# Turning the data on TensorE instead of in the transfers, in a one-core S5 and H3 kernel

## The chip, the core and the metric

The kernel runs on one core of a Trainium2 chip. A core has five engines that each work through their own instructions in order: TensorE (PE, matrix products, with its weight loads listed apart as PEld), VectorE (DVE), ScalarE (ACT), GpSimd (POOL) and SyncE (SP), which here only issues transfers. Sixteen DMA engines carry the transfers. An engine waits for another only where a semaphore says so. Data lie in SBUF (128 partitions) or in PSUM, where TensorE puts its results. The metric is the device time of one execution in microseconds (us); lower is better. The kernel before took 339.0 us, the median of three runs (338.59 to 339.09).

## What is computed

Two kinds of layer alternate on a tensor `x` of 2048 tokens by 640 channels. `_layernorm` has no weights.

```python
def _A_ref(x, Lambda_re, Lambda_im, B_re, B_im, C_re, C_im, log_dt, Dskip):
    ...
    Lam_bar = jnp.exp(dt * Lam)
    Bu = jnp.einsum("bld,pd->blp", x + 0j, B_bar)
    for t in range(L):
        h = Lam_bar[None, :] * h + Bu[:, t, :]
        hs.append(h)
    y = 2.0 * jnp.einsum("blp,dp->bld", hseq, Cmat).real + x * Dskip[None, None, :]

def _B_ref(q, k, v, shift_k, ssm_k, ssm_D):
    for t in range(ks):
        k_shift = k_shift + k_pad[:, t:t + S, :] * shift_k[:, ks - 1 - t][None, None, :]
    kv = k_shift * v
    ...
    y_f = kv_f * kf_f[None, :, :, :]
    y = irfft2(y_f)[:, 0, :S, :] + kv * ssm_D[None, None, :]
    return q * y

x = A_x
x = x + _A_ref(_layernorm(x), ...)
x = x + _B_ref(_layernorm(x), B_k, B_v, B_shift_k, B_ssm_k, B_ssm_D)
x = x + _A_ref(_layernorm(x), ...)
x = x + _B_ref(_layernorm(x), B_k, B_v, B_shift_k, B_ssm_k, B_ssm_D)
```

The long convolution `y` of a B layer depends on k, v and the two filters alone, not on `x`. So the kernel computes it once, keeps it in DRAM (`ysd`), and both B layers multiply by it.

## The kernel before

**Order.** Nothing is scheduled while the kernel is being built. Each piece of work is a named task of the class `Sched` (`add`), and the string `ORDER` (lines 59 to 141) lists all 896 tasks in one order. `run` emits them so, and each engine gets its own tasks in that order. A suffix gives the engine where a task has a choice: `/a` ACT, `/d` DVE, `/p` POOL. `PLACE` (from line 143) fixes the address of each buffer in one large SBUF area, `arena`, and the PSUM banks. The times that tasks carry (`c_mm`, `c_act`, `c_tt`) are not used when the kernel is built.

**Set-up.** `y_table_tasks` (line 998) makes the sine and cosine tables `Cf`, `Sf`, `NSf` for the forward spectrum, and `Ci`, `Si` as their turned copies by two DMA transposes (line 1047). Two negated copies, `NSi` and `NCi` (lines 1051 and 1053), follow on DVE. `a_setup_tasks` makes the weights of the A layers. A warm-up of 18 matmuls (line 1468) comes first on TensorE.

**The convolution.** The 640 channels go in five blocks of 128 (`kb`, `qd`). `kv_tasks` (line 1142) loads a block of k with a DMA transpose (line 1209) and a block of v plainly (line 1198), forms the short shift filter on TensorE (line 1227) and multiplies by v on DVE (line 1243). `y_pass` (line 1249) then takes kv, turned by another DMA transpose (line 1329), and the filter `ssm_k` (line 1311), through stage A (line 1272) and stage B (lines 1294 to 1296), whose results are copied out of PSUM by `evac` (line 290 on ACT, line 292 on DVE). The spectra are multiplied on DVE (lines 1350 to 1354). For block 0, which `PW_PE` names, the last two of these four operations are left out, and TensorE does them by a doubled number of products. The inverse stage (line 1376) uses `Ci`, `Si`, `NSi` as stationary operands and the spectrum as moving ones; its result `T` is turned by a DMA transpose (line 1389) into `TT`, TensorE applies `HA` (line 1404), and the block goes to `ysd` (line 1414).

**The A layers.** `ALayer.chunk` works on 512 tokens, four chunks per layer. After the layer norm, four `id` tasks (lines 696 and 698) write the normalised tokens in bf16, and one DMA transpose, task `tu` (line 726), turns them all. Tasks `bq` and `bp` (lines 750 and 765) multiply by B, `eq` and `ev` copy out of PSUM, `ri`, `sc` and `ro` (lines 803, 804, 820) run the recurrence on DVE, `hx` (line 875) takes a difference, `cp` (line 901) multiplies by C, and `xe` (line 909 on ACT, line 911 on DVE) adds up and gives the new `x`. Where `xe` is on ACT, TensorE adds the residual as well.

**The B layers.** `b_chunk` (line 917) normalises (`u`), multiplies by `ysd` (`mm`, line 959) and adds (`m`, lines 948, 980, 982). The last chunk of the last layer goes in four groups of one quarter; the output is stored after each second quarter (line 930).

Of the kernel before, what the change touches and what calls it, by code (L numbers as in the profile page):

```python
# [17 lines left out]
P = 128  # L18
L = 2048
# [18 lines left out]
PW_PE = (0,)  # L38
PW_PARTS = 1
VN = 1  # L40
KVS = ()
# [18 lines left out]
a_ldB1 a_ldB0 yt_io8 yt_ph8 kv_dsl kv_kd yq0_kl a_pl a_ti yt_h0 yt_io0 kv_pd2/p yt_f0 kv_lk0 kv_k0 yt_ph0 yt_f2 kv_d0  # L60
kv_lv0 warm kv_k1 a_b01:2 yt_sin8 xl0 yq1_kl kv_lk1 a_p0 kv_lv1 yt_sin0 yt_f3 a_b0e1:2/a a_p1 a_b00:4 a_b00:2 yt_neg8
kv_pd4/d kv_k2 yt_f4 kv_pd0/p a_p2 yq0_ka a_b0e0:4/a a_b01:3 yq0_KA:m0 a_b0e0:2/a a_p3 a_b00:3 a_b0e1:3/d yq0_KA:e0/d
kv_pd3/d kv_d1 kv_d2 a_p4a a_p4 kv_ds0 kv_ds1 a_dd yt_h1 kv_ds4 kv_ds3 kv_ds2 a_b00:1 a_b0e0:3/a a_b0e0:1/a a_b01:0
yt_neg0 a_b0e1:0/a a_b00:0 a_b0e0:0/a yq0_KA:m3 yq0_KA:e3/a yq0_KA:m2 kv_mm0:1 yq0_KA:e2/d kv_pd1/d a_ta yq0_KA:m1
a_b01:4 yq0_KA:e1/a kv_mm0:0 a_b0e1:4/a kv_ev0:1 a_t0 kv_ev0:0 yq0_vl a_ldC0 xl2 a_ldC1 a_p5a a_p5b yq0_KB:m0
yq0_KB:e0/a yq0_KB:m2 yq2_kl yt_Ci kv_lk2 yq0_KB:e2/a yt_Si a_p6 kv_lv2 yq1_ka a_f A1c0_ln_bn:1/d a_lamd/d yq1_KA:m1
yq1_KA:e1/a xl1 yq1_KA:m2 yq0_KB:m3 yq1_KA:m3 kv_mm1:0 yq1_KA:e3/a a_b01:1 yq1_KA:e2/a yq0_KB:e3/a kv_ev1:0 yt_h2
a_b0e1:1/a yt_h3/p a_t1 kv_mm1:1 kv_ev1:1 a_b11:3 yq0_VA:m2 a_b1e1:3/d yq0_VA:e2/d a_b11:0 a_b1e1:0/d a_b10:1
a_b1e0:1/d yq0_KB:m1 a_b11:1 a_b1e1:1/a yq0_KB:e1/d a_b11:4 yq0_VA:m1 yq0_VA:e1/a a_b1e1:4/d yq0_VA:m3 yq0_VA:m0
yq0_VA:e3/d yq1_KA:m0 yq0_VA:e0/a a_b10:4 a_t2 A1c0_ln_bn:2/d A1c0_ln_bn:3/d A1c0_ln_bn:0/d yq1_KA:e0/a a_b1e0:4/a  # L70
yq0_VB:m0 yq0_VB:e0/a a_ct1 yq0_VB:m3 a_wc01:0 a_wm01:0 yq0_VB:m2 yq0_VB:e3/a yq0_VB:e2/a a_wc01:1 A1c0_ln_sd a_b10:2
# [12 lines left out]
A1c3_ln_bn:3/d A1c3_ln_bn:1/d A1c3_ln_bn:2/d yq2_KB:e1/a yq1_IB:m3 yq1_IB:e0/a yq1_IB:e3/a a_ct3 a_wc03:0 a_wm03:0
yq1_IB:m1 yq1_IB:e1/a yq1_IB:m2 yq1_IB:e2/d a_wc03:1 a_wm03:1 yq3_ka yq2_KB:m2 A1c1_id:2/a yq2_KB:e2/a A1c3_ln_sd
yq1_tt kv_mm4:1 yq2_KB:m3 kv_ev4:1 A1c1_id:3/a yq2_KB:e3/a yq3_KA:m3 yq3_KA:m0 yq3_KA:e0/a yq3_KA:e3/d yq4_kl
yq2_VB:m0 yq2_VB:m3 yq2_VB:m2 yq2_VB:e0/d yq2_VB:e3/d yq3_KA:m2 A1c0_bq:2 A1c3_ln_post yq2_VB:e2/d yq3_KA:e2/a
kv_mm4:0 yq3_KA:m1 A1c0_eq:2/a yq2_VB:m1 A1c0_bp:2 yq3_KA:e1/a kv_ev4:0 A1c1_tu yq2_VB:e1/d yq2_pw:0 yq1_IA:m1
yq3_VA:m0 A1c0_ev:2/a yq3_VA:e0/a yq1_IA:e1/a A1c0_bq:1 A1c0_eq:1/a yq3_VA:m2 yq3_KB:m0 yq3_VA:m1 A1c0_bp:1 A1c2_tu
yq3_KB:e0/a yq3_VA:e2/a yq3_VA:e1/a yq3_VA:m3 yq3_KB:m3 yq3_VA:e3/d yq4_ka A1c3_id:1/d A1c3_id:3/d yq3_KB:e3/d  # L90
A1c3_id:0/d A1c0_ev:1/a yq2_IB:m2 yq3_KB:m2 yq2_IB:m0 yq2_IB:e2/a yq3_KB:e2/a yq3_VB:m3 yq2_IB:e0/d yq3_VB:e3/a
yq1_IA:m0 yq1_IA:e0/d A1c3_id:2/a yq3_VB:m0 yq3_VB:m2 yq3_VB:e2/d yq2_IB:m1 yq4_KA:m2 yq3_VB:e0/a a_rq yq3_KB:m1
yq3_KB:e1/a yq2_IB:m3 yq2_IB:e1/d yq2_IB:e3/a yq3_VB:m1 yq1_st A1c3_tu yq3_VB:e1/d yq3_pw:0 yq2_tt yq4_vl A1c0_bq:0
yq4_KA:e2/a A1c0_eq:0/a yq4_KA:m3 A1c1_bq:0 yq4_KA:m0 yq4_KA:e3/a yq4_KA:m1 A1c0_bp:0 yq4_KA:e0/a yq4_KA:e1/a
A1c2_bq:2 yq4_KB:m1 A1c0_ev:0/a A1c0_ri yq3_IB:m3 a_rq2 A1c0_sc A1c0_cy A1c0_ro A1c0_hx A1c1_eq:0/a yq4_KB:e1/a
A1c1_bq:2 yq2_IA:m0 A1c2_eq:2/a yq3_IB:e3/a A1c2_bp:2 yq2_IA:m1 yq2_IA:e0/a A1c2_ev:2/a A1c1_eq:2/a yq2_IA:e1/a
A1c1_xr A1c0_xr yq2_st A1c1_bq:1 yq4_KB:m2 A1c1_bp:2 A1c1_eq:1/a A1c1_bp:1 yq4_KB:e2/a A1c1_ev:2/a yq4_VA:m2 yq3_IB:m0
yq4_VA:e2/a A1c1_bp:0 yq3_IB:e0/a A1c1_ev:1/a yq4_KB:m3 A1c1_ev:0/a yq3_IB:m1 yq4_VA:m3 yq4_KB:m0 yq4_KB:e3/a
yq4_VA:e3/d yq4_KB:e0/d yq3_IB:e1/a A1c2_bq:0 A1c1_ri A1c1_sc A1c1_cy yq4_VA:m0 yq4_VA:m1 yq4_VA:e1/a A1c2_eq:0/a
A1c2_bq:1 yq3_IB:m2 yq4_VA:e0/a yq3_IB:e2/a A1c2_eq:1/a A1c2_bp:0 A1c2_ev:0/a yq4_VB:m3 yq4_VB:m2 A1c2_bp:1 yq4_VB:m0  # L100
yq4_VB:e2/a A1c2_ev:1/a yq4_VB:m1 yq4_VB:e3/a yq4_VB:e1/a A1c0_cp:1 A1c0_xe:1/a yq4_VB:e0/d yq4_pw:0 a_w10:2 yq3_tt
a_w10:1 a_w11:4 a_w1e0:2/a a_w11:0 A1c0_cp:3 a_w1e0:1/a a_w1e1:0/a a_w1e1:4/a a_w10:3 yq4_IB:m2 A1c0_xe:3/d A1c1_ro
A1c2_ri A1c2_sc a_w1e0:3/a yq4_IB:e2/a a_w10:0 a_w1e0:0/a a_w11:3 a_w1e1:3/a yq4_IB:m0 yq4_IB:e0/a a_w11:2 a_w1e1:2/a
yq4_IB:m1 yq4_IB:e1/a a_w10:4 yq4_IB:m3 a_w11:1 A1c1_cp:3 yq4_IB:e3/a a_w1e0:4/a a_w1e1:1/a yq3_IA:m0 yq3_IA:m1 yq4_tt
A1c0_cp:0 A1c1_xe:3/d A1c0_xe:0/d a_lamd2/a yq3_IA:e0/a yq3_IA:e1/a A1c3_bq:2 A1c3_eq:2/d A1c0_cp:2 A1c0_xe:2/d yq3_st
yq4_IA:m0 yq4_IA:m1 yq4_IA:e0/d yq4_IA:e1/a yq4_st A1c2_xr A1c3_bp:2 B1l0 A1c1_hx A1c1_cp:1 A1c2_cy A1c2_ro
B1c0_ln_sq:3 B1c0_ln_sq:1 B1c0_ln_sq:0 B1c0_ln_sq:2 B1c0_ln_sd B1c0_ln_post B1c0_u:3/a B1c0_u:1/a A1c3_e2:2/a
A1c1_cp:0 A1c1_xe:0/d A1c1_cp:2 B1c0_u:0/a A1c1_xe:1/d A1c1_xe:2/d B1c0_u:2/d B1c1_ln_sq:3 B1c1_ln_sq:2 B1c1_ln_sq:1
B1c1_ln_sq:0 A1c3_bq:0 B1c1_ln_sd A1c3_eq:0/a B1c0_mm A1c3_b4:2 A1c3_bq:1 A1c2_cp:1 B1c0_m:2 B1c0_m:0 B1c0_m:3
B1c0_m:1 A1c3_bp:0 B1c1_ln_post A1c3_eq:1/d A1c3_ev:2/d A2c0_ln_sq:1 A2c0_ln_sq:3 A2c0_ln_sq:0 A2c0_ln_sq:2 A2c0_ln_sd  # L110
B1l2 A1c3_xr B1l1 A1c2_hx B1c1_u:2/d A1c2_xe:1/d A1c3_bp:1 A1c2_cp:3 A2c0_ln_post A2c0_id:3/d A2c0_id:1/d A2c0_id:0/d
A2c0_id:2/a B1c1_u:0/a B1c1_u:3/d B1c1_u:1/d B1c1_mm B1c1_m:3 A1c3_e2:1/a B1c1_m:0 B1c1_m:1 B1c1_m:2 A1c2_xe:3/d
A1c3_b4:1 A1c3_e2:0/a A1c3_b4:0 A1c2_cp:2 A1c3_ev:1/a A1c3_ev:0/a a_tq/a A1c3_ri A2c0_tu A2c1_ln_sq:1 A2c1_ln_sq:3
A2c1_ln_sq:2 A2c1_ln_sq:0 A1c2_cp:0 A1c2_xe:2/d A1c2_xe:0/d A2c0_bq:0 A2c0_bq:2 A2c0_bq:1 A2c0_eq:0/a B1c2_ln_sq:0
A2c1_ln_sd A1c3_sc A1c3_ro A2c1_ln_post A2c1_id:0/d A1c3_hx:1 B1c2_ln_sq:2 B1c2_ln_sq:1 B1c2_ln_sq:3 B1c2_ln_sd
A2c0_eq:1/a A2c0_bp:0 B1c2_ln_post B1c2_u:3/d B1c2_u:0/d B1c2_u:1/d A2c0_eq:2/a A2c1_id:1/a A2c1_id:2/a B2l1 A1c3_h1:2
A1c3_h1:0 A1c3_eh:0/a A1c3_h1:1 A1c3_eh:1/a A1c3_eh:2/a B1c2_u:2/d B1c2_mm B1c2_m:0 B1c2_m:3 A2c0_bp:1 A2c0_bp:2
A2c1_id:3/a A2c0_ev:0/a A2c0_ev:1/a A2c0_ev:2/a A2c1_tu B1l3 A1c3_cp:3 A1c3_cp:2 A1c3_hx:0 B1c2_m:1 B1c2_m:2
A2c2_ln_sq:2 A2c2_ln_sq:3 A2c2_ln_sq:1 A2c2_ln_sq:0 A2c2_ln_sd A2c0_ri A1c3_xe:3/d A2c2_ln_post A1c3_xe:2/d
A2c2_id:3/a A2c2_id:0/a A2c2_id:1/a A1c3_cp:0 A1c3_cp:1 A1c3_xe:0/d A2c2_id:2/a A1c3_xe:1/a B1c3_ln_sq:0 B1c3_ln_sq:2  # L120
# [1439 lines left out]
```

## Time and profile before

| what | value |
|---|---|
| median of three runs | 339.0 us (338.59 to 339.09) |
| the profiled execution's own time | 339.59 us |
| its span, first to last instruction | 337.4 us |
| mean granted TensorE clock | 0.98 |
| DMA packets | 105,097, of which 97,885 are under 512 bytes; 41.61 MB |
| transposing transfers issued by SP | 20 from SBUF to SBUF, 5 from DRAM |

The profiled execution takes 2.2 us more than its span; that part lies outside the first and last instruction. "Busy" of an engine is the time in which at least one of its instructions is under way, waits left out. Consecutive matmuls overlap, and their ends are modelled, so a busy TensorE need not be working at its full pace. The granted clock falls to one half in two stretches, 3.4 us long from about 20 us and 6.8 us long from about 75 us.

### The profile page before, as it was taken

The page shows a single profiled execution, that of the slowest core. Times are in us where ns is not written, and L with a number is a line of the kernel's source. Part 1 is how long each engine was busy: PE and PEld are TensorE (multiplying, and loading weights), DVE is VectorE, ACT ScalarE, POOL GpSimd, SP SyncE. Part 2 cuts the span into 40 slices and gives each one's busy share as a digit, 9 for nine tenths or more (in the row PEclk, how much of TensorE's full clock was granted, in tenths as well). Part 3 has the DMA queues.
Part 4 walks back from the last instruction along what each step waited for, and adds up shares of the span by engine and source line. Part 5 has one row for each costly group of instructions (what it writes and reads, how often), then busy time and mean ns, then how long its engine had stood idle before and what let it go on. Part 6 is the DMA issues. An engine that isn't in the chain of part 4 may idle for free. (4 is left out here: it accounts for less than half of the span.)

```text
span 337.4 us, 8902 instructions
## 1 busy us (share of the span) xinstructions
PE 310.9 (92%) x3819; PEld 242.3 (72%) x3838; DVE 313.1 (93%) x477; ACT 253.4 (75%) x396; POOL 20.4 (6%) x51
## 2 busy tenths in 40 slices
PE   7678899868999999999998999999999999999991
PEld 3567688757888989887666678686685777775651
DVE  5999989989999799998998989999999999999996
ACT  5989999999967879665784687797885755482682
POOL 4496000000000000000000000000000000000000
PEclk9979999996999999999999999999999999999998
DMA  8999999899994683250645671404230260014014
GB/s 236 253 178 312 191 226 191 131 209 171 196 195 90 127 142 64 67 153 2 120 90 105 184 270 36 122 2 80 87 70 1 80 157 0 2 40 118 0 41 194
DMA packets 105097, 41.61 MB, mean 123 GB/s; under 512 B 97885, under 2 KB 100450, under 8 KB 105058
## 3 DMA queue, kind: packets, MB, share of 16 engines
q1 hardware_dynamic: 104912, 41.03, 56.0%
q8 instruction: 30, 0.49, 0.6%
q14 instruction: 9, 0.07, 0.1%
q10 hardware_dynamic: 146, 0.01, 0.0%
HBM read 19.02 MB, written 5.24 MB: 72 GB/s over the span
## 5 line engine op out<-in xcount | busy, mean ns | idle before, releaser
L290 ACT ACTIVATE arena<-banks 128x1024 bf16<-128x1024 f32 (+3 forms) x156 | 134.2, 910 | 43.7 <-PE banks L765 10.7
L901 PE MATMUL banks<-arena 128*128 128x128 bf16 (+1 forms) x782 | 98.5, 281 | 1.4 <-DVE arena L911 0.3
L901 PEld LDWEIGHTS <-arena 128*128 128x128 bf16 x800 | 59.7, 98 | 40.7 <-issue 2.1
L750 PE MATMUL banks<-arena 128*128 128x256 bf16 x400 | 46.5, 273 | 1.4 <-ACT arena L290 1.4
L765 PE MATMUL banks<-arena 128*128 128x256 bf16 x400 | 46.5, 273 | 0.0
L644 ACT ACTIVATE junk<-arena,sums 128x640 bf16<-128x640 f32 x48 | 39.6, 825 | 7.3 <-DVE arena L980 4.4
L750 PEld LDWEIGHTS <-arena 128*128 128x128 bf16 x400 | 38.4, 98 | 6.2 <-issue 1.6
L765 PEld LDWEIGHTS <-arena 128*128 128x128 bf16 x400 | 38.5, 98 | 4.4
L1294 PE MATMUL banks<-arena 128*128 128x256 bf16 x160 | 39.7, 286 | 1.4 <-ACT arena L290 0.9
L803 DVE TENSOR_TENSOR arena<-arena 128x5160 bf16<-128x5160 bf16 (+1 forms) x16 | 40.2, 2511 | 0.5
L696 ACT ACTIVATE arena<-arena,nmr,rstd 128x640 bf16<-128x640 f32 (+1 forms) x36 | 31.3, 915 | 12.0 <-DVE nmr L657 12.0
L292 DVE CAST arena<-banks 128x1024 bf16<-128x1024 f32 (+3 forms) x34 | 35.9, 1085 | 4.1 <-PE banks L1296 2.6
L820 DVE TENSOR_TENSOR_SCAN arena<-arena 128x1290 bf16<-128x1290 f32 (+1 forms) x16 | 39.3, 2500 | 0.2
L1295 PE MATMUL banks<-arena 128*128 128x128 bf16 x160 | 36.3, 227 | 0.0
L1296 PE MATMUL banks<-arena 128*128 128x128 bf16 x160 | 36.2, 227 | 0.0
L911 DVE SCALAR_TENSOR_TENSOR arena<-banks,arena 128x640 f32<-128x640 f32 x27 | 21.6, 819 | 3.2 <-PE banks L901 3.1
L1376 PE MATMUL banks<-arena 128*128 128x128 bf16 (+1 forms) x288 | 24.2, 237 | 0.4 <-DVE arena L493 0.4
L1376 PEld LDWEIGHTS <-arena 128*128 128x128 bf16 x288 | 20.7, 98 | 2.0 <-issue 0.5
L804 DVE TENSOR_TENSOR arena<-arena 128x2580 bf16<-128x2580 bf16 (+1 forms) x16 | 21.4, 1337 | 0.5
L1296 PEld LDWEIGHTS <-arena 128*128 128x128 bf16 x160 | 16.3, 102 | 2.5
L1295 PEld LDWEIGHTS <-arena 128*128 128x128 bf16 x160 | 16.3, 102 | 2.0 <-issue 1.9
L1294 PEld LDWEIGHTS <-arena 128*128 128x128 bf16 x160 | 16.3, 102 | 1.2 <-issue 0.2
(205 smaller groups left out, 406.6 us busy)
## 6 DMA issues: line engine op xcount, KB each, us to landing
arena<-in_A_x_dram SPq DMA_DIRECT2D x8, 640.0 KB, 7.3
arena<-ysd SPq DMA_DIRECT2D x8, 640.0 KB, 4.5
arena<-in_B_ssm_k_dram SPq DMA_DIRECT2D x5, 512.0 KB, 5.3
arena<-in_B_v_dram SPq DMA_DIRECT2D x5, 512.0 KB, 5.9
ysd<-arena SPq DMA_DIRECT2D x5, 512.0 KB, 4.0
out_dram<-arena SPq DMA_DIRECT2D x8, 320.0 KB, 2.2
arena<-in_A_B_im_dram SPq DMA_DIRECT2D x1, 800.0 KB, 4.9
arena<-in_A_B_re_dram SPq DMA_DIRECT2D x1, 800.0 KB, 6.8
```

The lines of the kernel that those rows point to most:

```text
L290: nc.scalar.activation(out, in_, ACT.Copy)
L292: nc.vector.tensor_copy(out, in_)
L644: nc.scalar.activation(small.junk, src(q), ACT.Square, bias=sums()[:, i:i + 1], scale=-float(D), accum_out=st["ssq"][:, i:i + 1])
L750: nc.tensor.matmul(pb[:, jj, c2, :], lhsT=bt0[:, c2, k, j * P:(j + 1) * P], rhs=uT[:, 2:4, k, :], start=(c2 == k == 0), stop=(c2 == 1 and ...
L765: nc.tensor.matmul(pb[:, jj, c2, :], lhsT=bt1[:, c2, j, k, :], rhs=uT[:, 0:2, k, :], start=False, stop=(c2 == 1 and k == NJ - 1), skip_gro ...
L803: nc.vector.tensor_tensor(tt, gs[:, :, None].to_broadcast([P, 2, 2, n]), by_pairs(tab.get().rearrange("p i j b -> p (i j b)"), n), ALU.mult)
L820: nc.vector.tensor_tensor_scan(gv, rt, gv, 0.0, ALU.mult, ALU.add)
L901: nc.tensor.matmul(pc[:, o0:o1], lhsT=lh, rhs=rh, start=(n == 0), stop=(n == len(ops) - 1))
L1294: nc.tensor.matmul(ps[:, g], lhsT=T["Cf"].get()[:, q, :], rhs=A[:, 2 * q:2 * q + 2, :], start=True, stop=False, skip_group_check=True)
L1295: nc.tensor.matmul(ps[:, g, 0, :], lhsT=T["Sf"].get()[:, q, :], rhs=aim, start=False, stop=False, skip_group_check=True)
L1296: nc.tensor.matmul(ps[:, g, 1, :], lhsT=T["NSf"].get()[:, q, :], rhs=are, start=False, stop=True, skip_group_check=True)
L1376: nc.tensor.matmul(ps[:, bi + b0:bi + b1, :], lhsT=T[tb].get()[:, q, :], rhs=rh, start=(n == 0), stop=(n == len(ops) - 1), skip_group_chec ...
```

## The change

**All 25 transposing transfers go.** TensorE turns the data in blocks of 128 by 128 into PSUM as bf16, and ACT or DVE copies them out.

```diff
-        def e_tu(_):
-            nc.sync.dma_start_transpose(out=s_uT.get().rearrange("p q k i -> p (q k) i"), in_=s_u.get())
+        for q in (1, 3, 0, 2):
+            s_pu = S.bank(f"{nm}_pu{q}", 1, lambda t: t.bitcast(BF)[:, 0:D])
+            def e_tu(_, slot=slot, s_pu=s_pu):
+                for k in range(NJ):
+                    nc.tensor.transpose(s_pu.get()[:, k * P:(k + 1) * P], s_u.get()[:, ...], aw["ident"][:])
+            def e_eu(eng, slot=slot, s_pu=s_pu):
+                evac(nc, eng, s_uT.get()[:, slot].rearrange("p k e -> p (k e)"), s_pu.get())
```

`bq` now waits for quarters 1 and 3 alone, `bp` for 0 and 2. In the same manner, with eight blocks to a PSUM bank and copies of 1024 elements:

```diff
-            nc.sync.dma_start_transpose(out=s_kT.get()[:, KPAD:KPAD + L], in_=B_k[0][:, kb * P:(kb + 1) * P])
+                for a in range(8):
+                    nc.tensor.transpose(s_pt.get()[:, a, :], s_in.get()[:, 8 * h + a, d0:d0 + P], consts["ident_bf"][:])
...
-            nc.sync.dma_start_transpose(out=s_xv.get(), in_=s_kv.get())
+                for o in range(8):
+                    nc.tensor.transpose(s_pt.get()[:, o, :], s_kv.get()[:, ...], T["id"][:])
...
-            nc.sync.dma_start_transpose(out=T[a].get(), in_=T[b].get().rearrange("p q k -> p (q k)"))
+                for q in range(8):
+                    nc.tensor.transpose(s_pt.get()[:, q, :], T[nm].get()[:, 8 * h + q, :], consts["ident_bf"][:])
```

| turned | matmul tasks | blocks | copies | elements of a copy |
|---|---|---|---|---|
| tokens (`tu`, `eu`), 8 chunks | 32 | 160 | 32 | 640 |
| k (`tk`, `ek`), 5 blocks | 10 | 80 | 10 | 1024 |
| kv (`tv`, `vl`), 5 blocks | 10 | 80 | 10 | 1024 |
| tables (`yt_t`, `yt_e`) | 4 | 32 | 4 | 1024 |

k and v are loaded plainly, two blocks of channels in one transfer (`KG`, `VG`: blocks 0 and 1, 2 and 3, then 4).

**Inverse spectrum.** The tables are one buffer `TI` (negated sine, cosine, sine). The spectrum is now the stationary operand and the tables move, so that the result comes out turned, and the rest of the turn is a store to DRAM (`ts`) and a load with another pattern (`tt`), 1 MB each.

```diff
-                    ops = [("Ci", Z[:, q], 0, 2), ("NSi", Z[:, q, 1, :], 0, 1), ("Si", Z[:, q, 0, :], 1, 2)]
-                    if split: ...
+                    nc.tensor.matmul(ps[:, b], lhsT=Z[:, q, 0, :], rhs=TI[:, q, 1:3, :]..., start=True, stop=False, ...)
+                    nc.tensor.matmul(ps[:, b], lhsT=Z[:, q, 1, :], rhs=TI[:, q, 0:2, :]..., start=False, stop=True, ...)
...
-            nc.sync.dma_start_transpose(out=s_TT.get(), in_=s_T.get().rearrange("p u s e -> p (u s e)"))
+        def e_ts(_):
+            nc.sync.dma_start(out=tsd[qd][:, :], in_=s_T.get().rearrange("p s i -> p (s i)"))
+        def e_tt(_):
+            nc.sync.dma_start(out=s_TT.get(), in_=rows(tsd[qd][:, :]))
```

`PW_PE` and `NCi` go; block 0 does all four spectrum operations on DVE like the others. The index tables for `HA` follow the new order of rows.

**Smaller edits.** The warm-up is 52 matmuls of 176 columns instead of 18 of 512. The last chunk stores each quarter by itself.

**A new `ORDER`, 995 tasks, and a new `PLACE`.** Counted from the two orders, the tasks with a choice of engine stand so (number on DVE, the rest on ACT or POOL):

| tasks | on DVE before | on DVE after |
|---|---|---|
| stage A of the filter (`KA`), of 20 | 3 | 7 |
| stage B of the filter (`KB`), of 20 | 3 | 6 |
| stage A of kv (`VA`), of 20 | 5 | 3 |
| last stage (`IA`), of 10 | 2 | 1 |
| `eq`, `ev`, `eh` of the A layers | 4 | 9 |
| `id`, of 32 | 12 | 14 |
| `bn`, of 16 | 16 | 15 |
| `xe`, of 32 | 27 | 28 |
| `u`, of 28 | 12 | 13 |
| copies of turned weights (`a_b`, `a_w`) | 6 | 5 |
| `a_lamd` | 1 | 0 |
| new `eu`, of 32 | | 5 |
| new `ek`, `vl`, `yt_e`, of 24 | | 7 |

SP's order at the start was the two matrices B, the first filter block, k, v, tokens; now it is k (1 MB), a matrix B, the other, tokens, the first filter block, two more token chunks, v.

## The prediction, made before the changed kernel was run

> **What bounds the kernel now.** I read the busy shares first.
>
> ```profile
> PE 310.9 (92%) x3819; PEld 242.3 (72%) x3838; DVE 313.1 (93%) x477; ACT 253.4 (75%) x396; POOL 20.4 (6%) x51
> ```
>
> DVE and PE are both above 90%, so the second view is the same by stretch (columns: window, its length, then busy us and instructions of each engine, clock, DMA share, GB/s).
>
> ```profile
> 0.00:10.00 10.00, 6.83 (x25) 2.85 (x25) 5.78 (x33) 6.25 (x9) 3.64 (x17) 1.00 0.91 231
> 10.00:90.00 80.00, 66.59 (x1383) 58.02 (x1382) 75.26 (x154) 76.17 (x104) 16.80 (x34) 0.94 1.11 208
> 90.00:190.00 100.00, 98.30 (x1217) 80.35 (x1220) 91.44 (x82) 72.66 (x100) 0.00 (x0) 1.00 0.52 106
> 190.00:330.00 140.00, 138.63 (x1195) 100.72 (x1208) 136.47 (x207) 96.19 (x179) 0.00 (x0) 1.00 0.27 74
> 330.00:337.40 7.40, 0.56 (x7) 0.36 (x4) 4.16 (x7) 2.10 (x6) 0.00 (x0) 0.79 0.57 221
> ```
>
> DVE is idle 24.3 us in all: 4.2 in the first 10 us, 3.2 in the last 7.4 (the final store), and inside 4.7, 8.6 and 3.5 in the three middle stretches, 16.8 together. The chain of waits agrees: its last 84 us are DVE work almost without a break. So DVE is the bound, with PE close behind. The DMA engines are full until 90 us and half empty after.
>
> Third, whether the turning transfers cost anything today. In the list of waits, most of their results are never waited for; the last turn of the convolution is:
>
> ```profile
> PEld L1404 <- DMA arena<-arena: 0.9, 1, 0.9
> PE banks L1404 <- DMA arena<-arena: 0.8, 1, 0.8
> ```
>
> This is one wait of PE of 0.9 us (weight load and matmul show it twice). No wait of DVE in the list is for turned data. So what is removed is nearly free for the engines, and what replaces it is engine work. Its prices (line, engine, forms, count, busy us, mean ns, idle):
>
> ```profile
> L290 ACT ACTIVATE arena<-banks 128x1024 bf16<-128x1024 f32 x113 | 110.9, 1025 | 27.1 <-PE banks L1272 7.6 <-PE banks L750 5.0 <-DVE arena L911 4.4
> L292 DVE CAST arena<-banks 128x1024 bf16<-128x1024 f32 x25 | 30.1, 1219 | 3.7 <-PE banks L1296 2.6 <-PE banks L1272 0.8 <-PE banks L1404 0.2
> L290 ACT ACTIVATE arena<-banks 128x640 bf16<-128x640 f32 x14 | 9.3, 704 | 0.5 <-PE banks L508 0.5
> L292 DVE CAST arena<-banks 128x640 bf16<-128x640 f32 x6 | 4.8, 816 | 0.4 <-PE banks L524 0.2
> ```
>
> **DVE, the sum that decides.** Consecutive instructions overlap by about 0.08 us (two 128x1024 casts in a row take 2.36, one 1.22), so each counts its mean less 0.08: 1.14 for a copy of 1024, 0.74 for 640.
>
> *Moved tasks*, from the table of engines: KA, KB, VA, IA together four more copies, 4 x 1.14 = 4.6; `eq`, `ev`, `eh` 4.4 (two more of 1024, four more of 512 at 0.61, one of 256 at 0.34 less); `id` 0.6; `xe` 0.75; `u` 0.5; weight copies -0.7; `bn` -1.0; `a_lamd` -2.1 (its twin, one 128x1920 product, took 2.1); three memsets -0.15. Together **6.8**.
>
> *New copies*: 5 of 640 and 7 of 1024. At the f32 rows they cost 5 x 0.74 + 7 x 1.14 = 11.7. Those rows read f32 from PSUM, the new ones bf16. The Trainium skill, "VectorE: DVE Perf Modes", section "Why PSUM operands drop a tier", says that a PSUM source still allows two elements a cycle if it is 16-bit, and one if fp32. By that rule I estimate 0.60 and 0.40, that is 6.2. The trace has no 16-bit read from PSUM; in SBUF its bf16 product of 5160 takes 2843 ns, about 0.55 ns an element against 1.0 in the f32 copy. I take the rule, **6.2**, and keep 11.7 for the range.
>
> *Block 0's spectrum*: two more 128x2048 operations, 2 x 1.14 = 2.3; the negated cosine table (0.68) goes. **+1.6**.
>
> DVE thus grows by 6.8 + 6.2 + 1.6 = 14.6 (20.1 at f32 rates), to **327.7 us busy** (333.2).
>
> **PE.** The price of a turned block is read from products with the identity, which already turn the weights:
>
> ```profile
> 10.02 1.07 PE L508 MATMUL banks<-ident_bf,arena 128*128 128x128 bf16 x15
> ```
>
> Less the 0.22 us of the last one's latency, that is 0.057 us each. 160 + 80 + 80 + 32 = 352 blocks cost 19.7 us. Block 0's doubled products go: 16 x (0.109 + 2 x 0.056) = -3.5, with 0.109 from eleven 256-column matmuls that start 1.09 us apart; one `xe` of the second A layer leaves PE, -1.5. Net +14.7. In the inverse stage, two products of 256 columns replace one of 256 and two of 128: nothing. The warm-up has 9152 columns instead of 9216: nothing. By start-to-start times, PE's present work is 1254 x 0.056 + 1086 x 0.109 + 341 x 0.216 and some 30 us of smaller shapes, 292 us, so 307 after. It stays under DVE, but has no slack from 90 us on.
>
> A rule speaks against the change here. The row says 0.057 us at a granted clock of 1.00. The same skill, "TensorE: Matmul & The Clock Gate", section "Part 4: PE-mode transpose", says that work in transpose mode does not count as activity for the clock gate, so that full rate does not engage. By the row PE gains 19.7 us, by the rule, were every turn at half rate, 39.4. The trace's clock fell to a half in 70 to 80 us, where PE was busy 6.32 of 10. But the turns come five or eight at a time, under half a microsecond, among dense matmuls. I take the row and keep up to 10 us for the range.
>
> **ACT.** 44 of the 56 new copies: 27 x 0.63 + 17 x 0.94 = 33, less what it gives to DVE, net about +29: 282 of some 350 us. It was idle 84; hidden in sum, though each copy now stands between two PE tasks in place of a transfer. Of this lengthened chain PE to ACT to PE I keep +1 us (between 0 and 5).
>
> **Transfers.** SP loses 25 transposing issues that held it 2 to 6 us each, which frees the queue for the loads behind them. The roundtrip through DRAM is priced from
>
> ```profile
> arena<-in_B_ssm_k_dram SPq DMA_DIRECT2D x5, 512.0 KB, 5.3
> ysd<-arena SPq DMA_DIRECT2D x5, 512.0 KB, 4.0
> ```
>
> The new pair has 1 MB each: a store between 4.0 and 8.0, a load with the filter's pattern between 5.3 and 10.6; I take 5.5 + 8 = 13.5 us (from nearly half as much again as the rows, since part of a transfer is fixed), against the 8.3 to landing of one turn today. `tt` waits on SP for `ts`, and behind it stand only later loads. Blocks 0 to 3 have tens of us of other work between. For block 4, PE has five `cp` tasks between `tt` and `IA`, about 3 us each (10 x 0.216 + 15 x 0.056): 15 us cover 13.5. Cost nothing, and 5 us if the cover fails. The k and v loads in pairs have longer rows and fewer issues: nothing on a path. At the start, the first filter block now stands behind 3.3 MB of other loads, about 14 us at the 231 GB/s of the first window, so stage A begins later than today's 11.5; DVE has norms and k copies to do instead.
>
> **What relief the DMA engines give.** Until 90 us PE waits behind transfers, afterwards DVE waits behind PE: 8.6 us idle in 90 to 190. With the turns gone, PE work can move forward. Between none and all of the 8.6, I take half, -4.3. In the last 140 us nothing is to be gained: there the second A layer adds 80 blocks, 4.5 us, to a PE busy 138.6 of 140.
>
> **Sum.** DVE 327.7 + ends 7.4 + inside 16.8 - 4.3 + 1 = 348.6 us of span. The profiled execution took 2.2 more than its span, 350.8; the median of the runs shown is 0.6 under the profiled one: **350.2 us**, 3.3% slower. With f32 copies 355.7, with no relief 354.5, with both 360.0; with all of the relief 346.
>
> **Rivals.**
>
> *Faster: the transfers were the bound of the first 90 us.* PE did only 54 us of paced work there, and the order can now be packed densely. Place: the gaps of DVE between 10 and 330 us. Price: at most the 16.8 of them. It decides only if less than 2.3 us of them remain: with 1.5, 327.7 + 7.4 + 1.5 + 1.6 = **338.2**. For it: DMA share 1.11 in that window. Against it: DVE was busy 75.26 of those 80 us anyway, and at f32 copies even zero gaps give 342.
>
> *PE becomes the bound*, by the clock rule or because it was already dense. 307 us plus what PE leaves unused today (337.4 - 292 = 45) give a span of 352; half of the 10 us that I kept for the clock makes 357, a time of **358.6**. Against: clock 1.00 in all dense stretches.
>
> *The roundtrip of block 4 is late.* Both B layers wait for it; today the store lands at 191.1 and the load is issued at once, so this path is nearly tight. Five us on the forecast: **355**. For: the load of `ysd` has a wait of 2.3 us for that store. Against: `cp` work lies before it.
>
> *The change buys nothing but costs little*: if the new order hides even DVE's growth by dense packing, but not below today: 339 to 344.
>
> **Chances.** Forecast 344 to 356: 0.62. PE bound or clock: 0.14. Roundtrip late beyond 356: 0.07. Between 339.7 and 344: 0.08. A measurement can't tell 0.2%, 0.7 us, from no change: within it 0.03. Faster: 0.06. The range of 8 in 10 runs from 342.5 to 361. Slower by over 0.2%: 0.91.
>
> **What would show it.** DVE busy near 328 us says the sum is right, 333 that bf16 copies run at the f32 rate: the 1024 copies on DVE would then take 1.2 us instead of 0.66. The turned blocks should start 0.056 us apart, with the clock at 1.00 from 90 us on. PE's waits for `TT` in the `HA` stage should stay under 2 us. DVE's idle time should be near 20 us. The forecast is wrong if DVE's busy time does not rise by over 10 us, or if its idle time leaves the 12 to 30 us that the bounds allow.

## The result, and the profile after

The changed kernel takes **365.7 us** (median of four runs, 364.73 to 365.88) beside 338.8 for the kernel before on the same chip: a ratio of 1.079, with an interval of 1.077 to 1.081. It is 7.9% slower, where 3.3% was forecast; the time lies outside the forecast's 344 to 356 us. The profiled execution spans 363.9 us.

First the busy shares of the changed kernel.

```profile
PE 331.8 (91%) x4092; PEld 263.7 (72%) x4092; DVE 329.3 (90%) x496; ACT 280.9 (77%) x447; POOL 17.6 (5%) x54
```

Then the same stretches as before the change (window, its length, busy us and instructions of PE, PEld, DVE, ACT, POOL, then clock, DMA share, GB/s).

```profile
0.00:10.00 10.00, 8.24 (x76) 8.11 (x77) 6.75 (x35) 5.69 (x9) 6.26 (x26) 1.00 0.84 252
10.00:90.00 80.00, 63.07 (x1250) 54.33 (x1249) 70.44 (x148) 74.92 (x116) 11.34 (x28) 0.91 0.53 145
90.00:190.00 100.00, 94.41 (x1256) 80.18 (x1252) 86.75 (x75) 79.35 (x94) 0.00 (x0) 0.98 0.42 113
190.00:330.00 140.00, 140.00 (x1308) 104.93 (x1307) 135.65 (x193) 105.87 (x192) 0.00 (x0) 1.00 0.23 71
330.00:363.90 33.90, 26.06 (x217) 16.14 (x214) 29.68 (x48) 15.04 (x36) 0.00 (x0) 0.93 0.21 77
```

The sums of work are where the forecast had them: DVE busy 329.3 us (327.7 forecast), ACT 280.9 (282). The DMA engines are relieved, from a share of 1.11 to 0.53 in the second stretch. But DVE is idle for 363.9 - 329.3 = 34.6 us instead of 20.9, and PE, which was to move forward, did less from 10 to 90 us: busy 63.07 of 80 us against 66.59, though it now has the turned blocks to do as well.

What was added costs what it was priced at. The rows of the copies and turns in the changed kernel (line, engine, forms, count, busy us, mean ns, idle):

```profile
L306 DVE COPY arena<-banks 128x1024 bf16<-128x1024 bf16 x7 | 4.7, 673 | 3.1 <-PE banks L1368 1.9 <-PE banks L1255 1.2
L306 DVE COPY arena<-banks 128x640 bf16<-128x640 bf16 x5 | 2.4, 486 | 0.4 <-PE banks L746 0.4
L304 ACT ACTIVATE arena<-banks 128x640 bf16<-128x640 bf16 x27 | 18.5, 705 | 0.8 <-PE banks L746 0.8
L304 ACT ACTIVATE arena<-banks 128x1024 bf16<-128x1024 bf16 x17 | 17.2, 1031 | 0.4 <-PE banks L1255 0.4
L746 PE MATMUL banks<-ident_bf,arena 128*128 128x128 bf16 x160 | 12.9, 219 | 0.5 <-ACT arena L304 0.5
```

The 219 ns are one turned block from start to end; within a group of five the blocks start 0.056 us apart (median), as priced.

So the time went into waiting. To see whose, I cut each trace at 120 us. Of the kernel before, then of the changed kernel:

```profile
0.00:120.00 120.00, 103.42 (x1866) 86.97 (x1867) 107.48 (x209) 104.89 (x141) 20.44 (x51) 0.96 1.00 193
120.00:330.30 210.30, 207.23 (x1956) 155.27 (x1972) 201.77 (x264) 146.38 (x250) 0.00 (x0) 1.00 0.32 80
```

```profile
0.00:120.00 120.00, 95.72 (x1766) 83.65 (x1767) 103.32 (x212) 107.65 (x161) 17.60 (x54) 0.93 0.55 148
120.00:356.20 236.20, 235.80 (x2329) 179.98 (x2326) 221.98 (x279) 171.12 (x281) 0.00 (x0) 1.00 0.26 78
```

After 120 us PE is busy to the last in both kernels. (Before it shows 207.23 of 210.30, but there 1956 matmuls stand against 1972 weight loads: some matmul records are missing.) DVE, whose work ends the chain of waits, is idle for 8.5 and 14.2 us there. **PE is the bound from 120 us on in both**, and the end is 120 us, plus the work of PE that is left then, plus a tail. This can be made a ledger. I count each matmul at the pace at which its kind starts in dense stretches (0.056, 0.109 and 0.216 us for 128, 256 and 512 columns, the rarer shapes likewise). It is an estimate. "Gaps" is what it leaves over: the start of the last matmul, less 120 us, less the work left. That this is 0.6 us in 236 speaks for the count.

| us | before | after | difference |
|---|---|---|---|
| PE's work by pace, whole kernel | 296.3 | 310.2 | +13.9 |
| of it done by 120 us | 86.5 | 74.6 | -11.9 |
| left at 120 us | 209.8 | 235.6 | +25.8 |
| gaps of PE after 120 us | 0.5 | 0.6 | |
| last matmul starts at | 330.3 | 356.2 | +25.9 |

(The kernel before lacks 19 matmul records; its 296.3 is read from run e11 below, which has the same PE program with all 3838.) Of the loss of 27 us, 25.8 are thus **13.9 us of more work for PE and 11.9 us less of it done in the first 120 us**. In that front the work is late early on. By the timelines (start, us, then as above) the first spectrum product starts at 46.3 us before and at 63.8 after:

```profile
46.27 2.29 DVE L1350 TENSOR_TENSOR arena<-arena 128x4096 bf16<-128x4096 bf16 x1 [0.54 <-ACT arena L290]
63.76 2.29 DVE L1392 TENSOR_TENSOR arena<-arena 128x4096 bf16<-128x4096 bf16 x1
```

### The profile page after: what moved, and what is told of

The parts are those of the page before. It is cut to its first block, busy times and chain, and to the rows that moved or that the text cites. A ratio compares the mean times of both kernels' runs of the same rounds, so it can differ in the third digit from the quotient of the medians.

```text
span 363.9 us, 9512 instructions
## 1 busy us (share of the span) xinstructions
PE 331.8 (91%) x4092; PEld 263.7 (72%) x4092; DVE 329.3 (90%) x496; ACT 280.9 (77%) x447; POOL 17.6 (5%) x54
## 5 line engine op out<-in xcount | busy, mean ns | idle before, releaser
L304 ACT ACTIVATE arena<-banks 128x1024 bf16<-128x1024 f32 (+5 forms) x193 | 161.7, 891 | 44.6 <-PE banks L885 9.5
L925 PE MATMUL banks<-arena 128*128 128x128 bf16 (+1 forms) x800 | 99.7, 283 | 0.0
L925 PEld LDWEIGHTS <-arena 128*128 128x128 bf16 x800 | 59.7, 98 | 39.4 <-issue 1.1
L306 DVE CAST arena<-banks 128x1024 bf16<-128x1024 f32 (+3 forms) x41 | 44.3, 1092 | 9.9 <-PE banks L1306 3.4
L789 PE MATMUL banks<-arena 128*128 128x256 bf16 x400 | 46.6, 273 | 0.0
L774 PE MATMUL banks<-arena 128*128 128x256 bf16 x400 | 46.3, 273 | 0.0
L774 PEld LDWEIGHTS <-arena 128*128 128x128 bf16 x400 | 38.5, 98 | 4.7
L789 PEld LDWEIGHTS <-arena 128*128 128x128 bf16 x400 | 38.5, 98 | 4.4
L710 ACT ACTIVATE arena<-arena,nmr,rstd 128x640 bf16<-128x640 f32 (+1 forms) x33 | 29.4, 917 | 13.3 <-DVE nmr L671 7.8
L1328 PE MATMUL banks<-arena 128*128 128x256 bf16 x160 | 37.2, 274 | 1.9 <-DVE arena L306 0.9
L1329 PE MATMUL banks<-arena 128*128 128x128 bf16 x160 | 35.1, 219 | 0.0
L1330 PE MATMUL banks<-arena 128*128 128x128 bf16 x160 | 35.0, 219 | 0.0
L935 DVE SCALAR_TENSOR_TENSOR arena<-banks,arena 128x640 f32<-128x640 f32 x28 | 22.5, 819 | 2.1 <-ACT junk L658 1.2
L1408 PE MATMUL banks<-arena 128*128 128x256 bf16 x80 | 19.4, 284 | 3.0 <-DVE arena L1277 1.9
L1409 PE MATMUL banks<-arena 128*128 128x256 bf16 x80 | 19.5, 284 | 0.0
L1306 PEld LDWEIGHTS <-arena 64*128 64x128 bf16 x320 | 10.1, 95 | 11.0 <-issue 8.4
L1329 PEld LDWEIGHTS <-arena 128*128 128x128 bf16 x160 | 15.7, 98 | 3.1 <-issue 2.8
L1330 PEld LDWEIGHTS <-arena 128*128 128x128 bf16 x160 | 15.7, 98 | 1.9
```

Source lines behind the costliest of these rows:

```text
L304: nc.scalar.activation(out, in_, ACT.Copy)
L306: nc.vector.tensor_copy(out, in_)
L710: nc.scalar.activation(dst, src, ACT.Identity, bias=st["nmr"][:, i:i + 1], scale=st["rstd"][:, i:i + 1])
L774: nc.tensor.matmul(pb[:, jj, c2, :], lhsT=bt0[:, c2, k, j * P:(j + 1) * P], rhs=uT[:, 2:4, k, :], start=(c2 == k == 0), stop=(c2 == 1 and ...
L789: nc.tensor.matmul(pb[:, jj, c2, :], lhsT=bt1[:, c2, j, k, :], rhs=uT[:, 0:2, k, :], start=False, stop=(c2 == 1 and k == NJ - 1), skip_gro ...
L925: nc.tensor.matmul(pc[:, o0:o1], lhsT=lh, rhs=rh, start=(n == 0), stop=(n == len(ops) - 1))
```

## The experiments

Theory 1: PE is the bound from 120 us on, and the turns burden it. Theory A (C in the later runs): ACT holds the front back, loaded with the new copies. Theory B: the new order holds the front back, whatever the turns cost. Rivals: DVE is the bound; the roundtrip through DRAM; the clock. A run that takes tasks out or moves them also needed some other addresses (`PLACE`). The ledger of all runs ("time" is the median; "done" by 120 us and "gaps" of PE after it are of the one profiled execution, which in e16 was the slowest of 20, at 342.5 us, and in e17 the fastest of four, at 363.1; where some 20 records are missing, PE's work is that of the same program with all of them):

| run | time | PE's work | done | gaps |
|---|---|---|---|---|
| before / after | 338.8 / 365.7 | 296.3 / 310.2 | 86.5 / 74.6 | 0.5 / 0.6 |
| e1 tokens by DMA | 367.0 | 301.2 | 71.9 | 8.4 |
| e2 k, kv by DMA | 366.0 | 301.2 | 66.8 | 1.3 |
| e3 all turns by DMA | 374.2 | 290.5 | 56.5 | 9.8 |
| e4 second layer turned twice | 368.7 | 314.7 | 75.4 | 0.7 |
| e5 k, kv not turned | 360.5 | 301.2 | 71.0 | 0.3 |
| e10 280 blocks not turned | 359.7 | 294.5 | 67.6 | 4.3 |
| e9 order of the front changed | 368.1 | 310.2 | 71.3 | 1.6 |
| e13 ACT relieved | 361.6 | 310.2 | 78.2 | 0.2 |
| e14 = e13 and e5 | 360.5 | 301.2 | 70.9 | 0.4 |
| e15 no wait for the store | 364.7 | 310.2 | 74.7 | 0.5 |
| e17 DVE relieved | 364.5 | 310.2 | 76.8 | 0.5 |
| e18 = e14 and e17 | 359.3 | 301.2 | 71.6 | 0.4 |
| e6 old order, roundtrip | 364.8 | 292.6 | 76.2 | 20.0 |
| e7 old order, tokens on PE | 367.9 | 305.2 | 81.8 | 13.8 |
| e8 old order, kv on PE | 365.7 | 300.8 | 73.3 | 8.9 |
| e12 the same, other places | 356.2 | 300.8 | 76.7 | 2.6 |
| e11 old order, ACT dummies | 345.4 | 296.3 | 80.7 | 0.6 |
| e16 old order, ids on GpSimd | 340.0 | 296.3 | 83.8 | 0.6 |

### Undoing the turns in the new order

**e1, e2, e3.** Parts of the turns go back to transposing transfers, issued as soon as their data and their place in memory allow.

```diff
-                for k in range(NJ):
-                    nc.tensor.transpose(s_pu.get()[:, k * P:(k + 1) * P], s_u.get()[:, ...], aw["ident"][:])
+            nc.sync.dma_start_transpose(out=s_uT.get().rearrange("p q k i -> p (q k) i"), in_=s_u.get())
...
-                    nc.tensor.transpose(s_pt.get()[:, a, :], s_in.get()[:, 8 * h + a, d0:d0 + P], ...)
+            nc.sync.dma_start_transpose(out=s_kT.get()[:, KPAD:KPAD + L], in_=B_k[0][:, kb * P:(kb + 1) * P])
...
-                    nc.tensor.transpose(s_pt.get()[:, o, :], s_kv.get()[:, ...], T["id"][:])
+            nc.sync.dma_start_transpose(out=s_xv.get(), in_=s_kv.get())
```

> The changed kernel with one part undone: the tokens of both A layers are turned by one DMA transpose per chunk again; 160 blocks leave PE (160 x 0.056 = 9.0 us), 27 copies leave ACT, 5 leave DVE (5 x 0.40 = 2.0 us). Theory 1, PE is the bound from about 120 us on: the end follows PE, 356 to 359 us. Rival, DVE is still the bound, its 34.6 us of idle come from the order: only DVE's 2.0 us return, 362 to 365. Rival, the roundtrip of the inverse spectrum through DRAM is the delay: nothing returns, 364 to 367.

> The changed kernel with another part undone: k is loaded by a transposing transfer and kv is turned by one; 160 blocks leave PE (9.0 us), 13 copies of 1024 leave ACT and 7 leave DVE (7 x 0.60 = 4.2 us), nearly all of this before 110 us. Theory 1, PE is the bound after 120 us, and the copies on ACT and DVE held it back before: PE's 9.0 us and some us of the earlier front return, 348 to 357. Rival, DVE is the bound: 4.2 us return, 360 to 363. Rival, roundtrip: 364 to 367. If the transposing transfers were worth removing here, the time rises above 366.

> All 25 turns by transposing transfers again (tokens, k, kv, tables); the new order, the swapped roles of the inverse stage and the roundtrip through DRAM stay. 352 blocks leave PE (19.7 us), 44 copies leave ACT, 12 leave DVE (6.2 us). Theory 1: 338 to 347. Rival, the new order or the roundtrip makes the time: 358 or more. Rival, DVE is the bound: 358 to 360.

Measured: **367.0, 366.0 and 374.2 us**. Nothing came back, so theory 1 in its plain form fell. The ledger says why: PE has 9 us less to do in e1, but waits 8.4 us after 120 us. The list of PE's waits from 190 us on in e1:

```profile
PE banks L774 <- DMA arena<-arena: 5.4, 2, 3.9
```

A transfer of the second layer's tokens is not there when `bq` wants it, in an order that gives it no time. In e2 and e3 the front falls back (done 66.8 and 56.5). There the engines now wait for transfers: in the first 65 us of e2 DVE waits 2.6 us for the filter (0.5 in the changed kernel) and PE 2.5 us for a matrix B, in e3 DVE waits 6.8 us at one time for a turned table. These runs don't show that the turns on PE are free; they show that the new order does not fit the transposing transfers. In that order, turning everything on PE is 8.5 us faster than turning everything by transfer (e3).

**e4.** Each token block of the second layer is turned twice.

```diff
-                for k in range(NJ):
+                for k in [*range(NJ)] * (2 if self.lname == "A2" else 1):
```

> The changed kernel, each of the 80 blocks of the second A layer turned twice into the same place: 4.5 us more on PE between about 200 and 330 us, nothing on another engine. Theory 1: 369.5 to 371. Rival, DVE is the bound and PE has slack: 365.5 to 367.

Measured **368.7**, +3.0 for 4.5 us of work, between the two expectations and nearer to the first. PE has no gaps (0.7), so the blocks are paid; the front of the profiled execution happened to be 0.8 us further on, and its last matmul starts 3.8 us later. It also bears on the clock. In 10 to 40 us the changed kernel had a granted clock of 0.83, e4, whose front is the same program, 0.94. First the changed kernel's window, then e4's:

```profile
10.00:40.00 30.00, 21.73 (x466) 19.05 (x463) 28.81 (x70) 29.04 (x56) 11.34 (x28) 0.83 0.82 220
```

```profile
10.00:40.00 30.00, 20.23 (x471) 17.59 (x470) 28.75 (x70) 29.00 (x56) 11.09 (x28) 0.94 0.83 222
```

By 65 us both had done the same work (37.3 and 37.2 us by pace), so the lower clock cost nothing there. Of the changed kernel's own executions, one at a mean clock of 0.970 took 365.64 us and one at 0.983 took 365.68. But in e17 below the time rises from 363.06 to 365.57 us as the mean clock falls from 0.982 to 0.965. The clock thus does not make the 27 us, yet a difference of 1 or 2 us between two runs can be its doing.

**e5, e10.** The turns are left out and nothing takes their place.

```diff
-        for h in range(2):
-            ...
-            t_vl.append(S.add(f"yq{qd}_vl:{h}", ...))
+        s_xv = s_kv
+        t_vl = list(evs)
```

> The changed kernel with the turning of k and of kv left out altogether: k is loaded plainly in a layout that needs no turn, and stage A reads kv as it is; no transposing transfer takes their place, so the output is not the reference's. 160 blocks leave PE (9.0 us), 13 copies leave ACT and 7 leave DVE, nearly all before 110 us. Theory A, ACT and DVE, loaded with these copies, hold the front of the work back in the first 65 us: the front comes forward and PE has 9 us less, 343 to 354 us. Theory B, the new order itself puts the steps of the convolution late, whatever the turns cost: 359 to 366.

> The changed kernel with 280 of its 352 turned blocks and their copies left out (k, kv, and the tokens of six of the eight chunks: all but chunks 0 and 1 of the first A layer; the tables stay), nothing in their place, so the output is not the reference's. PE has 15.7 us less. Theory 1, PE is the bound from 120 us on: 360.5 of the run without k and kv turns, less 120 blocks x 0.056 = 6.7, 353 to 355. Theory B, the order sets the rest: 358 to 361. Were the turns all of the loss: 345 or less.

Measured **360.5** and **359.7**. With 280 of 352 blocks and 44 copies gone, PE has less to do than in the kernel before (294.5 against 296.3), and the kernel is still 21 us slower. Of e10's 15.7 us of work, 7.0 stand against less done by 120 us, since the blocks turned there count as done in the changed kernel, and 3.7 against new gaps; 5.0 are left. So the larger part of the loss is not the turned blocks' own time. Nor is it their copies: in e5 nine copies of some 1 us each are gone from ACT ahead of the first spectrum product, and that product starts at 61.4 instead of 63.8 us. Both results lie in the ranges of theory B.

### What holds the front back

Up to the first spectrum product, before and after:

```profile
0.00:46.27 46.27, 36.04 (x636) 27.86 (x636) 39.67 (x117) 41.01 (x63) 20.44 (x51) 0.96 1.08 231
0.00:63.76 63.76, 48.89 (x827) 43.40 (x828) 55.03 (x155) 58.13 (x98) 17.60 (x54) 0.92 0.73 197
```

ACT works 41.0 us before and 58.1 after: 17.1 more, almost the 17.5 by which the product is late. Of it 11.9 are new copies, 4.4 `a_lamd` and 3.0 copies of B's weights; 3.7 us of other copies went to DVE. DVE has 15.3 more, 8.6 of them statistics of the first layer's norms, which the new order puts ahead.

**e11.** Dummies on ACT in the kernel before.

```diff
                 evac(nc, eng, s_S.get()[:, s0:s1, :, :].rearrange("p s c d -> p (s c d)"), ...)
+                if eng == "act" and qd == 0:
+                    nc.scalar.activation(JUNK[0], JUNK[0], ACT.Copy)
```

> The kernel before with 11 dummy copies of 640 on ACT, each put behind an ACT copy of block 0's spectra, some 0.6 to 0.7 us each, 7 us of ACT work before 46 us; nobody waits for their result. Theory A, ACT sets the pace of the front and the front sets the end: 344 to 347. Rival, the front has room on ACT, or the later stretches take the delay up: 338 to 341.

Measured **345.4**, ratio 1.018 (1.015 to 1.022): +6.3 us for 8.1 us of dummies, whose rows read

```profile
L1308 ACT ACTIVATE junk<-junk 128x640 bf16<-128x640 bf16 x7 | 5.2, 749 | 0.0
L1284 ACT ACTIVATE junk<-junk 128x640 bf16<-128x640 bf16 x4 | 2.9, 736 | 0.0
```

The first spectrum product is 5.2 us late, the start of the second layer 5.9, the end 5.9: what is lost in the front is never won back, because PE is full behind it.

**e9, e13, e14.** The changed kernel, with work taken out of the front's way.

```diff
-a_p6 ... a_lamd/a ... A1c1_id:3/a ... A1c1_id:0/a
+a_p6 a_lamd/p ... A1c1_id:3/p ... A1c1_id:0/p
...
+        if eng == "pool":
+            for i in range(15):
+                nc.gpsimd.tensor_tensor(to[:, i], ident[:], l[:, i:i + 1].to_broadcast([P, P]), ALU.mult)
```

This is e13; in e9 `a_lamd` goes to DVE and chunk 1's norm and `id` tasks stand behind `yq0_pw` in the order; e14 is e13 with e5's edit.

> The changed kernel with two pieces of its order changed: the product a_lamd goes from ACT (4.4 us there) back to DVE (2.0 us), and the layer norm of chunk 1 of the first A layer (four bn on DVE, its id tasks) is moved behind the first spectrum product, so that DVE has some 5 us and ACT some 6 us less to do ahead of it. Nothing is removed. Theory B (the order of the first 65 us sets the front): the spectrum product of block 0 starts 4 to 8 us before 63.8, and 3 to 7 us come back, 358 to 363. Theory 1 (only the sum of PE's work counts): 365 to 367.

> The changed kernel with work taken from ACT alone in the first 65 us: a_lamd (4.4 us on ACT) and two id tasks of the first A layer (0.9 us each) go to GpSimd, which is idle from 25 us on; nothing is put on DVE or PE. Theory C, ACT sets the pace of the front (8.1 us of dummy copies there cost the kernel before 6.3 us), and what is lost in the front is never won back: 3 to 5 us come back, 360.5 to 363. Theory B, ACT is only one of several in the way: 364 to 366.5. If the longer GpSimd work holds PE's a_b1 products up: above 366.5.

> The same relief of ACT, and in addition the turning of k and kv left out with nothing in its place (so the output is not the reference's). ACT then has about 16 us less ahead of the first spectrum product than the changed kernel, as much as it has more than the kernel before. Theory C: the front is that of the kernel before but for PE and DVE, 350 to 356. Theory B, DVE (8.8 us more of layer norms ahead of that product) or the order of PE's tasks takes ACT's place: 358 to 361.

Measured **368.1, 361.6 and 360.5**. e13 gives 4.1 us for 6.2 us taken from ACT, as theory C said. ACT's window from 10 to 70 us, in the changed kernel and then in e13 (length, busy us, clock, DMA share, GB/s):

```profile
10.00:70.00 60.00, 58.68 (x97) 0.91 0.65 172
```

```profile
10.00:70.00 60.00, 55.33 (x82) 0.97 0.65 173
```

So ACT was full there and did hold the front. But e14 is no better than e5 (360.45 and 360.46): a second limit stands close behind. And e9 is slower, outside both expectations: its first product starts 2.1 us earlier (61.7), but the norms that were moved then stand before the second one, which is 3.1 us late (94.6 against 91.5). Moving is not removing.

**e17, e18.** The statistics on DVE are left out, in the changed kernel and in e14.

```diff
-                for h in range(2):
-                    nc.vector.bn_stats(bs[:, h, :], x[:, h * (D // 2):(h + 1) * (D // 2)])
-                nc.vector.bn_aggr(mv[:, q, :], bs[:])
+                nc.vector.memset(mv[:, q, :], 0.5)
```

> The changed kernel with the 15 statistics tasks of the first A layer's norms that run on DVE left out (a constant is written in their place, so the output is not the reference's): DVE has some 13 us less ahead of the first spectrum product, ACT and PE as before. If DVE holds the front as much as ACT does: 355 to 362. If ACT alone (95 to 100% busy from 10 to 70 us) holds it: 364 to 366.

> All three reliefs together: k and kv not turned, a_lamd and two id tasks on GpSimd, and the 15 statistics left out. ACT then has about 16 us and DVE about 13 us less ahead of the first spectrum product. If ACT and DVE together are what holds the front: well below the 360.5 of the run with ACT's relief alone, 345 to 353. If the order of PE's tasks or the transfers hold it: 357 to 361.

Measured **364.5 and 359.3**: 1.2 us less either time, which is within the spread of the runs (e17's two executions at clocks of 0.967 and 0.965 took 365.16 and 365.57, one of the changed kernel at 0.970 took 365.64). DVE is not the second limit. The first 120 us of e18:

```profile
0.00:120.00 120.00, 92.82 (x1693) 80.27 (x1694) 90.96 (x179) 95.79 (x137) 24.87 (x71) 0.90 0.56 155
```

No engine is full here, and still only 71.6 us of PE's work are done. PE's waits in it are many and short, in turn for ACT, DVE and transfers, the longest 2.9 us. By elimination it is the sequence of the tasks, in which each engine waits for the next, or the addresses chosen with it, for a task also waits until its buffer is free: no run changes one without the other. Nor is it shown what part the clock has here, 0.90 beside 0.96 in the kernel before. Which step counts most stays open.

**e15.** The roundtrip.

```diff
-            nc.sync.dma_start(out=s_TT.get(), in_=rows(tsd[qd][:, :]))
+            nc.sync.dma_start(out=s_TT.get(), in_=rows(B_ssm_k[0:256, :]))
```

> The changed kernel, the load of the turned inverse spectrum reads 1 MB of an input in place of the DRAM buffer that was just stored, so that it does not wait for the store (the output is not the reference's). If the roundtrip delays the changed kernel: 355 to 362. If the order hides it, as PE's 2.5 us of waits for it suggest: 363 to 366.

Measured **364.7**, 1.0 less, within the spread of the runs (362.98 to 365.52). The roundtrip is hidden in the new order. The changed kernel's transfers (the last number is the median of us to landing), and then, in the list of waits of its first 120 us, the one wait that PE has for them:

```profile
tsd<-arena SPq DMA_DIRECT2D x5, 1024.0 KB, 5.0
arena<-tsd SPq DMA_DIRECT2D x5, 0.2 KB, 7.5
```

```profile
PE banks L1438 <- DMA arena<-tsd: 2.5, 1, 2.5
```

### Parts of the change in the old order

**e6, e7, e8, e12.** One part each in the kernel before, in this order: the inverse stage with its roundtrip; the tokens on PE; kv on PE, right behind its last multiplication; the same later.

```diff
-... kv_ev0:1 a_t0 kv_ev0:0 yq0_vl ...
+... kv_ev0:1 a_t0 kv_ev0:0 a_ldC0 xl2 a_ldC1 yq0_tv:0 yq0_tv:1 yq0_vl:0/a yq0_vl:1/a a_p5a ...
```

```diff
+... yq1_KA:m2 yq0_tv:0 yq0_tv:1 yq0_KB:m3 yq1_KA:m3 yq0_vl:0/a yq0_vl:1/a ...
```

The first of these is e8, the second e12.

> The kernel before, in its old order, with only the inverse spectrum changed: spectrum as stationary operand, result through DRAM (store and load of 1 MB per block) instead of a transposing transfer, all four spectrum operations of block 0 on DVE; the 20 other turns stay transposing transfers. If the roundtrip or the swap is what delays: 343 to 352. If it is hidden, as forecast: 336 to 341 (PE has 3.5 us less, DVE 1.6 more).

> The kernel before, in its old order, with only the tokens of both A layers turned on PE: 160 blocks (9.0 us of PE), 32 copies of 640 on ACT (20 us). If PE is full from 90 us on, its 9 us go to the end: 345 to 350. If DVE is the bound and PE and ACT have room: 338 to 342.

> The kernel before, in its old order, with only kv turned on PE: 80 blocks (4.5 us of PE), 10 copies of 1024 on ACT (9.4 us) before 130 us, where ACT is busy 95 of 100. Theory A (ACT and DVE hold the front back): 343 to 349. Theory B (only the order matters): 338 to 341.

> The same work as in the run with kv turned on PE in the old order, put at other places of the order: the turns where kv has long been written, the copies a few steps behind them. If the place in the order is what cost 27 us there: 342 to 352 (4.5 us of PE and 9.4 us of ACT remain). If turning kv on PE costs that much wherever it stands: 361 to 367.

Measured **364.8, 367.9, 365.7 and 356.2**. None lies in a range that was named. I had not expected that e6, e7 and e8 would each cost about as much as the whole change. e8 and e12 do the same work; the places in the order, with the banks and addresses to match, make 9.5 us. The work itself explains 4.5 us on PE and 9.4 on ACT of e12's 17.2. In e8 the lists of waits, of PE and of ACT, show the hand-over: the turn waits for kv, and ACT, which has other work behind it, waits for the turn.

```profile
PE banks L1336 <- DVE arena L1245: 1.9, 1, 1.9
ACT arena L291 <- PE banks L1336: 4.9, 2, 3.7
```

In e7, from 120 us on, PE's `cp` tasks wait for copies on ACT, which has 32 more of them in its queue:

```profile
PE banks L922 <- ACT arena L295: 9.0, 4, 3.7
```

In e6 the `HA` stage waits 6.8 us for the roundtrip in the whole execution (first line; 2.5 us in the changed kernel), and after 120 us the inverse stage waits, by the list for a load of tokens and for DVE. How the roundtrip leads to these waits was not traced.

```profile
PE banks L1405 <- DMA arena<-tsd: 6.8, 3, 4.7
PE banks L1375 <- DMA arena<-in_A_x_dram: 5.8, 1, 5.8
PE banks L1375 <- DVE arena L821: 2.9, 1, 2.9
```

So these four runs measure insertion into an order that had no place for it, more than the parts.

**e16.** A try for a faster kernel: the old order with the four `id` tasks of chunk 0 on GpSimd.

```diff
-A1c0_id:2/a A1c0_id:0/a ... A1c0_id:1/a A1c0_id:3/a
+A1c0_id:2/p A1c0_id:0/p ... A1c0_id:1/p A1c0_id:3/p
```

> The kernel before with the four id tasks of chunk 0 of the first A layer (0.92 us each, at 50 to 56 us on ACT) on GpSimd. Theory C, each us taken from ACT in the front comes back at the end: 335.5 to 338. If the front has a second limit there (DVE), or GpSimd gets in DVE's way: 338.5 or more.

Measured **340.0**, a ratio of 1.004 (1.002 to 1.005): slower by a little rather than faster. These tasks lie behind the first spectrum product at 46 us, ahead of which e11's dummies cost so much; that this is the reason is not shown. No version here beats the kernel before.

## Why the prediction was wrong, step by step

- **PE's growth: right.** 14.7 us forecast, 13.9 measured. Its absolute figures, 292 and 307, were some 4 us low, for 19 matmul records are missing in the trace they were summed from.
- **DVE's and ACT's growth: right**, within 2 us each. bf16 copies out of PSUM take 673 and 486 ns on DVE where f32 ones take 1216 and 816, so the rule of the Trainium skill that was taken for them ("VectorE: DVE Perf Modes", "Why PSUM operands drop a tier") holds.
- **The price of a turned block and the clock: right.** The blocks start 0.056 us apart, and the granted clock is 1.00 from 120 to 356 us, with the 80 turned blocks of the second layer among the work; the rule that was weighed there and not taken does not show. With 280 blocks fewer, e10's profiled execution has a mean clock of 0.957 beside 0.970.
- **The roundtrip: right.** 13.5 us forecast, 5.0 + 7.5 measured, hidden but for 1.0 us at most. The store of 1 MB took 5.0 us where one of 512 KB takes 4.0, so part of it is fixed, as assumed. PE's one long wait for it, 2.5 us, is over the 2 us that were named as a sign.
- **"DVE, the sum that decides": the wrong engine.** The span was summed as DVE's busy time plus its idle time, and the idle time inside was to fall to 13.5 us. It rose: 34.6 us in all instead of 20.9, over the 12 to 30 us that the prediction named as bounds. That 13.7, with 1.6 of DVE's sum, is the whole 15.3 us between the forecast span of 348.6 and 363.9. DVE's gaps come from another engine's lateness here, so they do not carry over. The windows that the prediction shows had it: PE 98.30 of 100 and 138.63 of 140 us. It even says that PE "has no slack from 90 us on", but draws no sum from that. By PE, 13.9 us had to be added to the 337.4 at once: 351.3. This is 2.7 of the 15.3 us, and alone it would have left the time inside the forecast.
- **The relief of -4.3, "With the turns gone, PE work can move forward": wrong, and this is the step that failed.** It carries the other 12.6 us. PE had done 11.9 us less by 120 us, not more. The transfers were relieved, but "Until 90 us PE waits behind transfers" does not hold: PE's list of waits in the kernel before has 0.8 us for a transfer up to 90 us. ACT was busy 76.17 of 80 us already from 10 to 90 us, and of its new copies, priced as "hidden in sum", 19 of 44, some 16 us, fell before 91 us. e11 and e13 show the price of work on ACT in the front: about 0.7 us at the end for 1 us. Relief of ACT brought 4.1 us back. The rest is left, by elimination, to the new order and its addresses (e14, e18), and which of its steps is open.
- **The rival "PE becomes the bound" had the mechanism, and a term mis-sized**: "what PE leaves unused today (45)". By the ledger the changed kernel leaves 363.9 - 310.2 = 53.7 us unused, where the kernel before leaves 41.1 (45 with the records that are missing). The rival took the unused time over unchanged; it grew by the lateness of the front. That its 358.6 came nearest is in part luck, for 5 us of it were a slow clock, and after 120 us the clock was 1.00.

## What to carry to other kernels

Find the engine that has no gaps until the end, and sum along it: what it still has to do at the point from which it is full, and what delays that point. An idle time taken from the old trace can't be added to another engine's busy time. In an order that is fixed per engine, engine work in place of a transfer brings a hand-over (PE to ACT to PE) where something ran beside everything. In these runs its price depended on its place in the order: the same turns of kv, 4.5 us of PE, cost 27 us at one place and 17 at another.

## What the runs showed of the hardware

- A 16-bit source in PSUM speeds up DVE and not ACT: DVE's copy of 1024 falls from 1216 to 673 ns, ACT's stays (1027 and 1031 ns; with 640 elements 697 and 705).
- GpSimd's `id` task of 128x640 took 870 ns in e13 and 1388 ns in e16, the same instruction, beside 927 ns on ACT. The profile's spans on GpSimd are rough, and the cause is open.
- The DMA engines' share fell by half (1.11 to 0.53 between 10 and 90 us) and no time came of it: in the kernel before, PE had waited 0.8 us for them in the first 90 us.
